# One GpSimd operation for the sum and one for the product of 1024 tokens, and a new order of all queues, in a gated recurrence with a gated convolution

## The chip, the cores and the metric

The kernel runs on one core of a Trainium2 chip. The metric is the device time of one execution in microseconds (us). TensorE is PE in the profile, VectorE DVE, ScalarE ACT, GpSimd POOL, SyncE SP; SPq is SyncE's queue, which issues the transfers.

## What is computed

The inputs are x, r_gate and i_gate, each of 4 sequences of 6336 tokens with 256 channels in float32. A linear recurrence with gates runs along each sequence; a gated linear unit with a causal convolution over 5 tokens follows.

```python
log_a = 8.0 * sigmoid(r_gate) * log(clip(sigmoid(a_param), 1e-6, 1 - 1e-6))
a_t = exp(log_a)
norm = sqrt(maximum(1 - a_t * a_t, 1e-6))
x_gated = norm * sigmoid(i_gate) * x
h = a_t[:, t] * h + x_gated[:, t]            # for every t; y[:, t] = h
gate = sigmoid(sum_k conv_w[k] * shifted(y, k))
out = (gate * (y @ w_val)) @ w_out
```

## The kernel before

The 25344 tokens are cut into windows (w) of 512 tokens, the last of 256, and the windows into chunks (c): chunks 0, 1 and 25 have one window of 512, chunk 26 the one of 256, and all others two, so that chunk c from 2 to 24 holds windows 2c-2 and 2c-1. Output is made by window; the last window is cut into windows 49 and 50 of 128.

Every piece of work is a word in one long list, `ORDER`, written out in the kernel. A word such as `sc.9.1` calls `op_sc(9, 1)`, and `@4,5` names the PSUM banks that it uses. Each engine does its words in the order of the list, one after the other; there is no other scheduling. The words of a chunk, in the order in which data flows:

- `lr`, `li`, `lx` (SyncE): load 512 KB of r_gate, i_gate or x of a window. Each ring has four windows, so a load waits until the window four places earlier was consumed.
- `ta.c`, `tb.c` (ScalarE): tanh of half of r and of i, in bfloat16. `tr.c.h` (TensorE) transposes the first for one half h of the channels, for two chunks at a time, and `ex.c.h` (ScalarE) makes the decays a_t from it.
- `sq.c.h` squares the decays on GpSimd; `sa` does the same on ScalarE. `rt.b.k` (ScalarE) takes the square roots for a batch of up to four chunks in one or two operations, since it needs another activation table: `rt.3` is for chunks 4 to 7, `rt.4` for 8 to 11, and so on; `rt.4.0` is for chunks 8 and 9. `rd` does this for chunk 0 on VectorE. `nt.c` (TensorE) transposes the roots.
- `pp.w` and `up.w` (GpSimd): tanh plus one, in place, and its product with x, for one window. In five windows `xp` (TensorE) and `uv` (VectorE, two instructions) do this instead.
- `xg.c` (VectorE) multiplies that by the root; `xt.c.h` (TensorE) transposes it; `sc.c.h` (VectorE) is the scan of the recurrence.
- `cv.w` (convolution), `vl.w` (x times w_val) and `ou.w` (output product) are TensorE's; `tg.w` (ScalarE) is the gate's tanh, `gv.w` (VectorE) the gate times the value. `cd.w` (VectorE) or `ca.w` (ScalarE) copies the output out of PSUM, and `st.w` (SyncE) stores it.

In the profile's lines: L310 is `ta`, L313 `tb`, L320 `pp`, L332 `up`, L346 `uv`, L373 `ex`, L381 `sq`, L389 `sa`, L406 `rt`, L441 `nt`, L452 and L456 `xg`, L466 `xt`, L499 `sc`, L511 `cv`, L518 `tg`, L526 `vl`, L531 `gv`, L541 `ou`, L549 `cd`, L551 `ca`, L562 `st`, L292 the loads.

Of the kernel before, what the change touches and what calls it, by code (L numbers as in the profile page):

```python
# [9 lines left out]
P = 128  # L10
CONV_K = 5
# [15 lines left out]
NU = 10  # L27
NRI = 4
NX = 4
# [20 lines left out]
xt.1.1@6 xt.2.1@0 sc.1.1 tg.0 li.9 sc.2.1 li.8 ex.4.1 vl.0@4,5 xt.2.0@1 tr.4.0@6,7 tb.4 gv.0 sq.5.1 cv.1@2,3 sc.2.0  # L50
ex.4.0 li.11 pp.5 lx.7 xp.4@4,5 lx.6 pp.6 uv.4 ta.6 pp.7 nt.3@6,7 up.5 ou.0.0@0,1 ta.7 lr.14 cv.3@4,5 cd.0.0 li.10
sq.5.0 lx.9 xg.3 tg.3 cv.2@0,1 lr.15 tg.1 lx.8 st.0 vl.1@6,7 sq.4.1 tg.2 xt.3.1@4 gv.1 tb.5 tr.6.0@0,1 sc.3.1 up.7
tr.6.1@6,7 ex.6.0 vl.2@2,3 up.6 lx.11 gv.2 li.12 ou.1.0@4,5 ex.6.1 lr.17 cd.1.0 xt.3.0@2 lr.16 sq.4.0 lx.10 sc.3.0
li.13 tb.6 ou.2.0@6,7 sq.7.0 vl.3@0,1 ta.8 li.15 cv.4@4,5 gv.3 sq.6.1 cd.2.0 tg.4 lr.18 ou.3.0@2,3 cd.3.0 sq.7.1
xp.8@0,1 lx.12 uv.8 rt.3.0 li.14 vl.4@2,3 st.1 sq.6.0 gv.4 lr.19 xp.9@6,7 uv.9 pp.11 lx.13 ou.4.0@2,3 rt.3.1 pp.10
cd.4.0 st.2 nt.4@6,7 up.10 xg.4 nt.5@0,1 xg.5 xt.4.0@4 up.11 lx.14 sc.4.0 xt.5.0@3 nt.6@6,7 tb.7 xt.4.1@2 sc.4.1
vl.5@0,1 ta.9 cv.5@4,5 li.16 pp.12 pp.13 xg.6 tg.5 lr.21 up.12 lr.20 tb.8 gv.5 li.17 tr.8.0@6,7 lx.15 sc.5.0 xt.6.1@0
up.13 lx.16 ex.8.0 xt.5.1@1 li.18 li.19 tr.8.1@4,5 sc.5.1 nt.7@2,3 pp.14 ex.8.1 st.3 ou.5.0@6,7 sq.9.0 st.4 ta.10 xg.7
cv.8@4,5 lx.17 up.14 cd.5.0 cv.6@2,3 tg.8 sc.6.1 xt.6.0@1 tg.6 pp.15 vl.6@4,5 ta.11 cv.7@2,3 sq.8.1 gv.6 cv.9@6,7 tg.7
lr.24 sc.6.0 up.15 lr.25 tb.9 st.5 ou.6.0@2,3 lr.23 tr.10.0@4,5 sq.8.0 cd.6.0 tg.9 vl.7@0,1 ex.10.0 st.6 gv.7 vl.8@2,3  # L60
lx.19 pp.16 xt.7.1@6 li.20 gv.8 xt.7.0@7 sq.9.1 tb.10 tr.10.1@0,1 sc.7.1 ou.7.0@4,5 sq.11.0 ex.10.1 cv.10@2,3 li.23
cd.7.0 tg.10 cv.11@0,1 sq.11.1 sc.7.0 st.7 ta.13 lr.22 lx.18 ou.8.0@4,5 li.21 pp.17 li.22 vl.9@2,3 tg.11 cd.8.0 sq.10.1
lr.29 gv.9 vl.11@4,5 sq.10.0 st.8 rt.4.0 gv.11 vl.10@0,1 ou.9.0@6,7 gv.10 up.17 cd.9.0 ou.10.0@0,1 rt.4.1 cd.10.0 up.16
ou.11.0@6,7 cd.11.0 st.10 nt.8@2,3 lr.28 pp.19 lx.21 xg.8 nt.9@0,1 lx.20 pp.18 xg.9 xt.8.1@3 cv.12@6,7 up.18 sc.8.1
ta.12 xt.8.0@5 up.19 tg.12 lr.26 sc.8.0 nt.10@2,3 lr.27 tb.11 st.9 tr.12.1@6,7 xt.9.1@1 xg.10 cv.14@4,5 ex.12.1 li.24
pp.20 li.25 sc.9.1 lx.22 pp.21 vl.14@2,3 lx.23 tg.14 cv.13@6,7 sq.13.1 tb.12 gv.14 vl.12@4,5 up.21 gv.12 tg.13
tr.12.0@0,1 li.26 st.11 vl.13@2,3 ex.12.0 li.27 pp.22 gv.13 ou.14.0@4,5 up.20 ou.12.0@6,7 cd.14.0 ta.15 ou.13.0@2,3
cd.12.0 xt.10.1@0 xt.9.0@1 ta.14 sq.12.1 lr.33 cd.13.0 cv.15@6,7 sc.9.0 tg.15 pp.23 lr.30 nt.11@4,5 lr.32 tb.13 up.22
lr.31 tr.14.0@2,3 lx.25 xg.11 st.12 tr.14.1@6,7 lx.24 ex.14.0 sc.10.1 cv.17@4,5 up.23 li.28 xt.10.0@1 tg.17 cv.16@2,3
st.13 sc.10.0 sq.14.0 ex.14.1 st.14 vl.17@4,5 pp.25 tg.16 lx.26 gv.17 vl.16@0,1 sq.15.1 tb.14 vl.15@6,7 gv.16 li.29  # L70
xt.11.0@2 gv.15 pp.24 cv.18@0,1 ta.17 sq.14.1 sc.11.0 ou.15.0@4,5 ta.16 ou.16.0@6,7 sq.12.0 cd.15.0 cv.19@2,3 tg.18
cd.16.0 st.15 xt.11.1@4 sq.13.0 tg.19 lr.37 lx.27 sc.11.1 li.30 vl.18@6,7 li.31 sq.15.0 ou.17.0@0,1 rt.5.0 gv.18
vl.19@4,5 up.25 gv.19 ou.18.0@6,7 cd.18.0 up.24 rt.5.1 ou.19.0@4,5 cd.17.0 nt.12@2,3 cd.19.0 pp.26 lx.28 nt.13@6,7
lx.29 xg.12 pp.27 cv.20@4,5 lr.36 st.17 up.26 xg.13 st.16 xt.12.0@3 tg.20 sc.12.0 tr.16.0@6,7 tb.15 up.27 lx.30
vl.20@0,1 lr.35 xt.12.1@4 lr.34 gv.20 ex.16.0 li.32 tr.16.1@2,3 li.33 pp.28 sc.12.1 st.18 nt.14@0,1 up.28 ex.16.1 lx.31
cv.21@6,7 xg.14 st.19 xt.13.1@5 tb.16 pp.29 sc.13.1 vl.21@2,3 sq.17.1 cv.22@0,1 tg.21 li.34 xt.13.0@4 li.35 tg.22 gv.21
pp.30 ou.20.0@6,7 ta.19 cv.23@0,1 sc.13.0 up.30 ca.20.0 vl.22@2,3 xt.14.0@5 up.29 tg.23 gv.22 ou.21.0@6,7 ta.18
cv.25@0,1 cd.21.0 sq.17.0 sc.14.0 tb.17 ou.22.0@2,3 lr.38 lr.39 tr.18.0@6,7 sq.16.0 st.20 lr.40 tg.25 cd.22.0 nt.15@4,5
# [31 lines left out]
def kernel(  # L110
# [80 lines left out]
    with tc.manual_schedule():  # L191
# [89 lines left out]
        def place(w, n):  # L281
            return w % n
# [327 lines left out]
```

## Time and profile before

| | us |
|---|---|
| three timed runs | 281.42, 281.95, 282.34; median 281.95 |
| span of the profiled execution | 279.6 |
| busy: DVE, ACT, PE, POOL | 258.2, 267.0, 243.8, 233.0 |
| DMA | 104.75 MB, mean 375 GB/s |

The profile gives the span of the profiled execution, from its first instruction to its last; its time as the timed runs measure it is not given apart. An engine's busy time is a mean over stages, so the stretches of the span are to be read beside it. A row of groups has the line, the engine, the operation and its shapes, the count, then busy us and mean ns of one, then the idle time of the engine before them and what ended it.

### The profile page before, as it was taken

What the parts mean: (1) busy time and instruction counts of PE and PEld (TensorE: products, weight loads), DVE (VectorE), ACT (ScalarE), POOL (GpSimd) and SP (SyncE); (2) the same over time, 40 slices, a digit from 0 to 9 for tenths busy, and PEclk for the clock granted to TensorE, in tenths of its full rate; (3) what the DMA queues carried; (4) which work ended last, traced back from release to release, by engine and by line L of the source; (5) the groups of instructions that cost most, each with busy time, mean ns of one, the idle gap of its engine ahead of it and who ended that gap; (6) DMA issues with size and microseconds to landing.
All of it is one profiled execution on the core that took longest, in us unless ns stands there. A gap on an engine that the chain in (4) does not pass through costs nothing. (4 is left out here: it accounts for less than half of the span.)

```text
span 279.6 us, 6233 instructions
## 1 busy us (share of the span) xinstructions
PE 243.8 (87%) x2493; PEld 164.9 (59%) x2493; DVE 258.2 (92%) x221; ACT 267.0 (96%) x187; POOL 233.0 (83%) x152
## 2 busy tenths in 40 slices
PE   2368999898799779999889999899999899999994
PEld 2143566456647466874566575666675756856563
DVE  5587797899999999899999999999999999999992
ACT  5999999999999999999999999999999999999754
POOL 1569679997999998999999999999999977984200
PEclk9998899999999999999999999999999999999999
DMA  7999999999999999999999999999999999742765
GB/s 275 411 405 385 388 409 409 413 409 409 419 408 417 415 414 416 413 416 409 420 413 341 415 420 414 414 411 420 416 363 407 420 378 400 286 176 92 283 263 194
DMA packets 29563, 104.75 MB, mean 375 GB/s; under 512 B 3287, under 2 KB 4062, under 8 KB 29534
## 3 DMA queue, kind: packets, MB, share of 16 engines
q1 hardware_dynamic: 29520, 104.35, 94.4%
q8 instruction: 19, 0.31, 0.4%
q14 instruction: 10, 0.08, 0.1%
q10 hardware_dynamic: 14, 0.01, 0.0%
HBM read 78.39 MB, written 25.95 MB: 373 GB/s over the span
## 5 line engine op out<-in xcount | busy, mean ns | idle before, releaser
L381 POOL TENSOR_TENSOR ering<-aring 128x1024 f32<-128x1024 f32 (+1 forms) x51 | 90.7, 1799 | 13.8 <-ACT aring L373 13.7
L332 POOL TENSOR_TENSOR uring<-tbring,xring 128x1024 bf16<-128x1024 bf16 (+1 forms) x45 | 95.5, 2139 | 3.2 <-DMA xring<-in_x_dram 1.7
L499 DVE TENSOR_TENSOR_SCAN yring<-aring,yring,banks 128x1024 bf16<-128x1024 f32 (+4 forms) x46 | 96.8, 2116 | 0.8 <-PE banks L466 0.7
L511 PE MATMUL banks<-yring,diag 64*64 64x512 bf16 (+6 forms) x1080 | 63.1, 362 | 3.8 <-ACT aring L373 1.1
L531 DVE SCALAR_TENSOR_TENSOR tgring<-tgring,banks 128x1024 bf16<-128x1024 bf16 (+1 forms) x51 | 59.4, 1178 | 6.1 <-PE banks L526 5.1
L320 POOL TENSOR_SCALAR tbring<-tbring 128x1024 bf16<-128x1024 bf16 (+1 forms) x45 | 46.3, 1040 | 10.3 <-ACT tbring L313 10.3
L541 PE MATMUL banks<-wo,tgring 128*128 128x256 bf16 x396 | 50.9, 273 | 4.4 <-DVE tgring L531 2.1
L373 ACT ACTIVATE aring<-banks,khf 128x2048 f32<-128x2048 bf16 (+3 forms) x32 | 52.9, 1689 | 0.2 <-PE banks L357 0.2
L526 PE MATMUL banks<-yring,wv 128*128 128x512 bf16 (+4 forms) x216 | 50.1, 361 | 2.7 <-DVE oring L549 1.0
L518 ACT ACTIVATE tgring<-banks 128x1024 bf16<-128x1024 f32 (+1 forms) x51 | 50.6, 1011 | 0.8 <-PE banks L511 0.6
L541 PEld LDWEIGHTS <-tgring 128*128 128x128 bf16 x396 | 42.3, 114 | 14.2 <-DVE tgring L531 5.8
L310 ACT ACTIVATE taring<-rring 128x2048 bf16<-128x2048 f32 (+2 forms) x27 | 47.9, 1785 | 1.7 <-DMA rring<-in_r_gate_dram 1.7
L313 ACT ACTIVATE tbring<-iring 128x2048 bf16<-128x2048 f32 (+2 forms) x27 | 48.1, 1782 | 0.0
L511 PEld LDWEIGHTS <-diag 64*64 64x64 bf16 x1080 | 29.4, 105 | 27.7 <-issue 12.5
L406 ACT ACTIVATE ering<-ering 128x4096 bf16<-128x4096 f32 (+3 forms) x14 | 43.6, 3157 | 0.1
L549 DVE COPY oring<-banks 128x1024 f32<-128x1024 f32 (+1 forms) x34 | 39.9, 1189 | 0.4 <-PE banks L541 0.4
L357 PE MATMUL banks<-ident_b,taring 128*128 128x128 bf16 x396 | 29.4, 230 | 8.5 <-ACT taring L310 4.5
L466 PE MATMUL banks<-ident,uring 128*128 128x128 f32 x198 | 30.3, 279 | 4.4 <-DVE uring L452 1.6
L357 PEld LDWEIGHTS <-taring 128*128 128x128 bf16 x396 | 26.0, 103 | 12.3 <-issue 6.3
L526 PEld LDWEIGHTS <-wv 128*128 128x128 bf16 x216 | 19.1, 97 | 23.8 <-issue 10.2
L466 PEld LDWEIGHTS banks<-ident,uring 128*128 128x128 f32 x198 | 21.9, 141 | 14.5 <-DVE uring L452 3.4
L441 PEld LDWEIGHTS banks<-ident,ering 128*128 128x128 f32 x184 | 24.2, 208 | 6.8 <-issue 3.0
(52 smaller groups left out, 160.0 us busy)
## 6 DMA issues: line engine op xcount, KB each, us to landing
rring<-in_r_gate_dram SPq DMA_DIRECT2D x49, 512.0 KB, 8.4
iring<-in_i_gate_dram SPq DMA_DIRECT2D x49, 512.0 KB, 9.0
xring<-in_x_dram SPq DMA_DIRECT2D x49, 512.0 KB, 9.4
out_dram<-oring SPq DMA_DIRECT2D x49, 512.0 KB, 9.0
oring<-in_moe_w_val_dram SPq DMA_DIRECT2D x1, 256.0 KB, 8.9
rring<-in_r_gate_dram SPq DMA_DIRECT2D x1, 256.0 KB
iring<-in_i_gate_dram SPq DMA_DIRECT2D x1, 256.0 KB, 6.5
xring<-in_x_dram SPq DMA_DIRECT2D x1, 256.0 KB
```

Source lines behind the costliest of these rows:

```text
L313: nc.scalar.activation(**tangent(c, tbring, NTI, iring, NII))
L332: nc.gpsimd.tensor_tensor(out=u, in0=t1, in1=xt, op=ALU.mult)
L357: nc.tensor.transpose(out=bank[:, o:o + P], in_=taring[:, place(w, NTR), j, h * P:(h + 1) * P], identity=ident_b[:])
L373: nc.scalar.activation(out=dst, in_=src, func=ACT.Exp, scale=khf[:, h:h + 1], bias=khf[:, h:h + 1])
L381: nc.gpsimd.tensor_tensor(out=e, in0=a, in1=a, op=ALU.mult)
L466: nc.tensor.transpose(out=out[:, o + q:o + wins[w] // 2:nq], in_=uring[:, w % NU, q, h * P:(h + 1) * P, :].rearrange("p d two -> p (d two) ...
L499: nc.vector.tensor_tensor_scan(out=yring[:, h, col:col + o1 - o0], data0=aring[:, h, a_at[c] + o0:a_at[c] + o1], data1=xT[:, o0:o1], initi ...
L511: nc.tensor.matmul(out=gp[oh * 64:oh * 64 + 64, h, a:b], lhsT=diag[half * 64:half * 64 + 64, h, k, :], rhs=yring[half * 64:half * 64 + 64, ...
L518: nc.scalar.activation(out=tgring[:, w % NTG, :, 0:outs[w]], in_=live.pop(("gp", w))[:, :, 0:outs[w]], func=ACT.Tanh, scale=0.5)
L526: nc.tensor.matmul(out=val[:, m, a:b], lhsT=wv[:, hk, m * P:(m + 1) * P], rhs=yring[:, hk, col:col + b - a], start=(hk == 0), stop=(hk == ...
L531: nc.vector.scalar_tensor_tensor(out=tgring[:, w % NTG, :, 0:outs[w]], in0=tgring[:, w % NTG, :, 0:outs[w]], scalar=1.0, in1=live.pop(("va ...
L541: nc.tensor.matmul(out=ops[:, j * D:(j + 1) * D], lhsT=gv[:, hk, j:outs[w]:J], rhs=wo[:, hk, :], start=(hk == 0), stop=(hk == H - 1))
```

## The change

In chunks 4, 6 to 24 (but not 5) the two sums `pp` and the two products `up` become one sum `pq.c` and one product `uq.c` over both windows, 2048 columns each. Chunks 1 to 3 and windows 8, 9, 48 and 49 keep the old words (chunk 5 is windows 8 and 9, done by `xp` and `uv` in both).

```diff
+        def op_pq(c):
+            w, k = cwins[c][0], len(cwins[c])
+            t = tbring[:, place(w, NTI):place(w, NTI) + k, 0:wins[w] // P, :].rearrange("p k j d -> p (k j d)")
+            nc.gpsimd.tensor_scalar(out=t, in0=t, scalar1=1.0, scalar2=1.0, op0=ALU.mult, op1=ALU.add)
+
+        def op_uq(c):
+            w, k = cwins[c][0], len(cwins[c])
+            nc.gpsimd.tensor_tensor(
+                out=uring[:, w % NU:w % NU + k].rearrange("p k q d two -> p (k q) two d"),
+                in0=tbring[:, place(w, NTI):place(w, NTI) + k].rearrange("p k (q two) d -> p (k q) two d", two=2),
+                in1=xring[:, w % NX:w % NX + k].rearrange("p k (q two) d -> p (k q) two d", two=2), op=ALU.mult)
```

The words `s_kt` and `s_diag` of the start are split into `s_ktp`, `s_ktd` and `s_dgp`, `s_dgc`, `s_dgd` with the same instructions. `op_vl` may use one bank for a short window. An `op_sb` is defined and not used. The three words `sa.21.1`, `sa.26.0` and `sa.26.1` become `sq`. `ca.20`, `ca.30`, `ca.50` become `cd`, and `cd.28`, `cd.40`, `cd.49` become `ca`.

The whole of `ORDER` is new, with its banks. All rings and their sizes, the chunks, the batches and the places of decays and squares stay. The stretch around chunks 3 to 8, before:

```
... tb.4 gv.0 sq.5.1 cv.1@2,3 sc.2.0 ex.4.0 li.11 pp.5 lx.7 xp.4@4,5 lx.6 pp.6 uv.4 ta.6 pp.7 nt.3@6,7 up.5 ou.0.0@0,1
ta.7 lr.14 cv.3@4,5 cd.0.0 li.10 sq.5.0 lx.9 xg.3 tg.3 cv.2@0,1 lr.15 tg.1 lx.8 st.0 vl.1@6,7 sq.4.1 tg.2 xt.3.1@4 gv.1
tb.5 tr.6.0@0,1 sc.3.1 up.7 tr.6.1@6,7 ex.6.0 vl.2@2,3 up.6 lx.11 gv.2 li.12 ou.1.0@4,5 ex.6.1 lr.17 cd.1.0 xt.3.0@2
lr.16 sq.4.0 lx.10 sc.3.0 li.13 tb.6 ou.2.0@6,7 sq.7.0 vl.3@0,1 ta.8 li.15 cv.4@4,5 gv.3 sq.6.1 cd.2.0 tg.4 lr.18
ou.3.0@2,3 cd.3.0 sq.7.1 xp.8@0,1 lx.12 uv.8 rt.3.0 li.14 vl.4@2,3 st.1 sq.6.0 gv.4 lr.19 xp.9@6,7 uv.9 pp.11 lx.13
ou.4.0@2,3 rt.3.1 pp.10 cd.4.0 st.2 nt.4@6,7 up.10 xg.4 nt.5@0,1 xg.5 xt.4.0@4 up.11 lx.14 sc.4.0 ...
```

and after:

```
... ou.1.0@0,1 sq.4.0 uv.4 tb.4 nt.3@2,3 cd.1.0 ou.0.0@6,7 sq.5.0 ta.6 cv.3@4,5 xg.3 st.1 pq.4 cd.0.0 xt.3.1@2 tg.3
cv.2@0,1 sc.3.1 ta.7 st.0 sq.4.1 lx.8 vl.3@4,5 li.10 li.11 xt.3.0@3 tg.2 lx.9 vl.2@6,7 gv.3 sq.5.1 tb.5 tr.6.0@0,1 gv.2
uq.4 sc.3.0 ex.6.0 tr.6.1@6,7 li.12 lr.16 ou.3.0@4,5 ex.6.1 cd.3.0 cv.4@2,3 ou.2.0@4,5 sq.7.0 lx.11 tg.4 st.3 vl.4@0,1
cd.2.0 tb.6 xp.8@6,7 sq.6.0 gv.4 st.2 lr.17 ou.4.0@2,3 sq.7.1 cv.5@0,1 rt.3.0 cd.4.0 uv.8 sq.6.1 xp.9@2,3 st.4 lr.15
lx.10 lr.14 li.13 pq.6 uv.9 lx.13 rt.3.1 nt.4@4,5 li.14 nt.5@2,3 xg.4 li.15 xg.5 xt.4.0@7 vl.5@4,5 lx.12 sc.4.0
nt.6@2,3 tg.5 uq.6 ta.9 gv.5 xt.4.1@7 xt.5.1@1 sc.4.1 ou.5.0@4,5 ta.8 cd.5.0 tb.7 cv.6@6,7 lr.19 xg.6 st.5 lr.18 tg.6
pq.7 lr.20 sc.5.1 vl.6@2,3 lr.21 tb.8 li.17 tr.8.0@6,7 lx.15 uq.7 gv.6 ex.8.0 xt.5.0@1 tr.8.1@4,5 sc.5.0 ou.6.0@2,3
ex.8.1 nt.7@6,7 xt.6.0@0 cd.6.0 sq.9.0 ta.10 cv.9@4,5 xg.7 st.6 lx.14 cv.7@2,3 sq.8.1 li.16 sc.6.0 tg.9 li.18 li.19
cv.8@6,7 ta.11 lr.23 lx.17 pq.8 xt.6.1@1 sc.6.1 tg.8 tr.10.0@4,5 lr.24 sq.8.0 tg.7 vl.7@6,7 ex.10.0 vl.8@2,3 gv.7 uq.8
tr.10.1@0,1 gv.8 ou.7.0@6,7 tb.9 ou.8.0@2,3 cd.7.0 vl.9@4,5 ex.10.1 cd.8.0 st.7 cv.11@6,7 sq.11.0 gv.9 st.8 xt.7.1@2
tb.10 li.20 lx.18 sc.7.1 cv.10@4,5 sq.9.1 lx.16 lr.25 tg.11 ou.9.0@0,1 tg.10 sq.10.1 cd.9.0 vl.10@2,3 vl.11@4,5 gv.10
st.9 sq.11.1 lx.19 xt.7.0@6 rt.4.0 lr.22 gv.11 ou.10.0@0,1 sq.10.0 cd.10.0 sc.7.0 ou.11.0@0,1 st.10 li.21 pq.9 rt.4.1
li.22 nt.8@4,5 xg.8 ...
```

More of the change, by code (lines that the diff above doesn't have):

```diff
@@ L50 @@
[L50 to L54, printed above, removed]
@@ L106 @@
+ca.48.0 vl.50@6 vl.49@1 gv.50 tg.49 st.48 ou.50.0@7 gv.49 cd.50.0 ou.49.0@5 st.50 ca.49.0 st.49
 """
@@ L381, in op_sq, with op_sb @@
             nc.gpsimd.tensor_tensor(out=e, in0=a, in1=a, op=ALU.mult)
+        def op_sb(c):
+            at, n = H * e_at[c], clen[c]
+            a = aring[:, :, a_at[c]:a_at[c] + n]
+            nc.gpsimd.tensor_tensor(out=ering[:, at:at + H * n].rearrange("p (h n) -> p h n", h=H), in0=a, in1=a,
+                                    op=ALU.mult)
         def op_sv(c, h):
```

134 lines of the change are left out of this document (71 added, 63 removed).

## The prediction

> **What bounds the kernel now.** I read the page's head first, then busy time by stretch, then who waited for whom, then the single instructions around the places that the new order moves.
>
> ```profile
> span 279.6 us, 6233 instructions
> PE 243.8 (87%) x2493; PEld 164.9 (59%) x2493; DVE 258.2 (92%) x221; ACT 267.0 (96%) x187; POOL 233.0 (83%) x152
> ```
>
> The profiled span is 279.6 us; the three timed runs have a median of 281.95. The 2.35 us between them I take as what lies around the span, and keep it. Below, a sum is made on the span and 2.35 is added. A difference under 0.3% (0.85 us) is what a measurement of this kernel can hardly tell from none.
>
> ```profile
> 20.00:40.00 20.00, 17.59 (x119) 9.78 (x118) 15.42 (x16) 19.94 (x12) 15.81 (x13) 0.91 1.03 392
> 40.00:80.00 40.00, 34.53 (x332) 23.91 (x331) 37.38 (x31) 39.76 (x25) 38.31 (x23) 1.00 1.03 411
> 80.00:240.00 160.00, 148.52 (x1605) 102.34 (x1604) 158.53 (x121) 159.77 (x106) 154.31 (x95) 1.00 1.02 407
> 240.00:260.00 20.00, 19.74 (x211) 12.68 (x210) 20.00 (x16) 19.93 (x22) 14.70 (x11) 1.00 0.49 174
> 260.00:280.00 20.00, 15.81 (x182) 10.43 (x182) 13.83 (x16) 10.89 (x13) 1.11 (x1) 0.97 0.58 230
> ```
>
> Columns: stretch, length, then PE, PEld, DVE, ACT, POOL busy, granted clock, DMA share, GB/s. From 80 to 240 us VectorE is idle for 1.5 us (160 - 158.53) and ScalarE for 0.2; the DMA engines are full as well (1.02) and ease only after 240. GpSimd, whose work the change cuts, has 5.7 us to spare there. Three resources are therefore full together, and GpSimd is not among them. VectorE's queue holds the same operations before and after (only which output copies it takes differs), so to end earlier the kernel must shrink VectorE's idle: 4.6 us in 20 to 40, 2.6 in 40 to 80, 1.5 in 80 to 240, and the tail.
>
> ```profile
> POOL ering L381 <- ACT aring L373: 13.7, 6, 6.6
> POOL tbring L320 <- ACT tbring L313: 10.3, 5, 4.1
> SPq L562 <- ACT oring L551: 27.2, 10, 5.3
> SPq L562 <- DVE oring L549: 22.0, 10, 10.3
> xring<-in_x_dram SPq DMA_DIRECT2D x49, 512.0 KB, 9.4
> DMA to landing us min/median/max: 3.6/8.9/10.9
> ```
>
> GpSimd waits for ScalarE, so it follows and does not lead. SyncE's queue (SPq) stood 49 us at stores (L562) for their copies; every load behind such a store waits too. A load of x takes 9.4 us to land at the median (last column), and any load between 3.6 and 10.9.
>
> **The change part by part.**
>
> ```profile
> L332 POOL TENSOR_TENSOR uring<-tbring,xring 128x1024 bf16<-128x1024 bf16 x44 | 94.3, 2161 | 2.8 <-DMA xring<-in_x_dram 1.3 <-PE banks L526 0.7
> L332 POOL TENSOR_TENSOR uring<-tbring,xring 128x512 bf16<-128x512 bf16 x1 | 1.2, 1180 | 0.4 <-DMA xring<-in_x_dram 0.4
> L320 POOL TENSOR_SCALAR tbring<-tbring 128x1024 bf16<-128x1024 bf16 x44 | 45.7, 1049 | 6.2 <-ACT tbring L313 6.2
> L320 POOL TENSOR_SCALAR tbring<-tbring 128x512 bf16<-128x512 bf16 x1 | 0.6, 620 | 4.1 <-ACT tbring L313 4.1
> L381 POOL TENSOR_TENSOR ering<-aring 128x1024 f32<-128x1024 f32 x45 | 84.6, 1900 | 6.2 <-ACT aring L373 6.1
> L389 ACT ACTIVATE ering<-aring 128x1024 f32<-128x1024 f32 x1 | 1.1, 1107 | 0.0
> L389 ACT ACTIVATE ering<-aring 128x256 f32<-128x256 f32 x2 | 0.9, 438 | 0.0
> L551 ACT COPY oring<-banks 128x1024 f32<-128x1024 f32 x16 | 16.4, 1025 | 4.3 <-PE banks L541 4.3
> L549 DVE COPY oring<-banks 128x1024 f32<-128x1024 f32 x33 | 39.4, 1213 | 0.4 <-PE banks L541 0.4
> L531 DVE SCALAR_TENSOR_TENSOR tgring<-tgring,banks 128x1024 bf16<-128x1024 bf16 x49 | 58.5, 1209 | 4.0 <-PE banks L526 3.6
> L499 DVE TENSOR_TENSOR_SCAN yring<-aring,yring,banks 128x1024 bf16<-128x1024 f32 x38 | 88.2, 2336 | 0.1
> L406 ACT ACTIVATE ering<-ering 128x4096 bf16<-128x4096 f32 x11 | 39.4, 3614 | 0.1
> ```
>
> *The merged operations.* From 512 to 1024 columns the product grows by 981 ns, the sum by 429. So 2048 columns should cost 2161 + 2 x 981 = 4.12 us and 1049 + 2 x 429 = 1.91 us; two of each now cost 4.32 and 2.10. That is 0.39 us a chunk, 7.8 us over 20 chunks, and at least nothing if 2048 columns cost just twice as much. It is off the path, since VectorE and ScalarE set the pace: I put 0 in the sum. If GpSimd were last ahead of an `xg`, 0.39 us would be won there.
>
> A rule speaks against even that saving. The Trainium skill, GPSIMD Engine Reference, section 3.1, gives 4497 ns for a two-input operation of 2048 columns in fp32; at that price the product of a chunk would lose 0.18 us instead of winning 0.20, and the cut on GpSimd would be about 0.2 us in all instead of 7.8. No row of this trace has a 2048-column product; the sum for the end would stay the same, since neither is on the path.
>
> *Squares.* Three squares go from ScalarE (`sa`, 1.11 + 2 x 0.44 = 2.0 us) to GpSimd: 1.90 for `sq.21.1`, and by length about 0.5 (an estimate from the same row) for each of the two of 256 columns. GpSimd's busy time should so go from 233.0 to about 228 (-7.8 + 2.9). ScalarE is full, but VectorE is equally full with unchanged work, so I take 0 of the 2.0 us; bound -2.0.
>
> *Copies.* Which of the output copies ScalarE takes changes (three against three, of equal sizes): no work is won or lost, VectorE carries one more copy, 1.21 us, until late and one less at the end.
>
> *Start.* `xp.0` now sits in banks 2,3, which `ex.2.0` frees first. But VectorE's list up to `xg.4` is the same set in both orders, and `xg.4` also needs `rt.3.0`:
>
> ```profile
> 54.27 1.94 ACT L310 ACTIVATE taring<-rring 128x2048 bf16<-128x2048 f32 x1
> 58.43 7.13 ACT L406 ACTIVATE ering<-ering 128x4096 bf16<-128x4096 f32 x2
> 51.63 9.31 POOL L381 TENSOR_TENSOR ering<-aring 128x1024 f32<-128x1024 f32 x5
> 63.77 2.35 DVE L452 TENSOR_TENSOR uring<-banks,uring 128x2048 bf16<-128x2048 bf16 x2
> ```
>
> The first row is `ta.8`, which moves behind `rt.3`: `rt.3` could run 1.9 us earlier, and `xg.4` (63.77) with it. But `rt.3.1` needs the last square (51.63 + 9.31 = 60.94), and GpSimd has the same squares, sums and products before that point. Bounds -1.9 and 0; I take -0.5, nearer to none because of that square.
>
> *Loads behind stores.* This is the part I give most weight. SyncE issues in order. Before, one store (`st.0`) stands ahead of `lx.10`; now five do (`st.1 st.0 st.3 st.2 st.4`), and `st.4` waits for `cd.4`. And `uq.6` needs `lx.10` and `lx.11` both, where the old products took one window each.
>
> ```profile
> 52.44 0.33 SPq L292 DMA_DIRECT2D xring<-in_x_dram  x1
> 58.60 1.35 DVE L346 SCALAR_TENSOR_TENSOR uring<-tbring,banks 128x512 bf16<-128x512 bf16 x2
> 61.25 1.39 DVE L346 SCALAR_TENSOR_TENSOR uring<-tbring,banks 128x512 bf16<-128x512 bf16 x2
> 102.77 2.35 DVE L452 TENSOR_TENSOR uring<-banks,uring 128x2048 bf16<-128x2048 bf16 x2
> ```
>
> `lx.10` is issued at 52.44 now. In the new order `cd.4` stands just ahead of `uv.8` and `uv.9` (1.35 + 1.39) and `xg.4` (63.77), so it ends near 61.0; with `st.4` and `lr.15` issued between, `lx.10` goes out near 62.0, ten us later. With a 9.4 us landing, `uq.6` (4.12) ends at 75.5. `xg.6` stands on VectorE behind `xg.4 xg.5` (2.35), two scans (2 x 2.34), `gv.5` and `cd.5` (2 x 1.21), about 9.1 us with the overlaps of some 0.08 each that the x2 rows show: 72.9. So `uq.6` is 2.6 us late; with the shortest landing, 3.6, it is 3.2 us early.
>
> The same happens at `lx.14`, now behind `st.6` and so behind `cd.6`: from 72.9, `xg.6`, two scans, `gv.6` and `cd.6` end near 80.8, `lx.14` goes out at 81.2. With 9.4 us, `uq.8` ends at 94.7. Behind it on GpSimd wait five squares, of which the second ends at 98.5 and releases `rt.4.0` (3.61): 102.1, and transposes still follow. `xg.8` is now at 102.77 and would be reached at 101.6, since one copy moved behind it: 0.5 late without the transposes, about 1.0 with them (my estimate); 0 with the short landing. ScalarE's own slack does not help there, because it waits for the squares.
>
> Together 0 to 3.6 us. While SyncE stands at a store fewer transfers are in flight, so the landing should fall below the median 8.9, yet 8.9 is nearer to what the trace shows most often than 3.6. At 7.5 us the first is 0.7 late and the second nothing; at 8.9, 2.1 and 0.5. I take 1.2.
>
> *Banks and the rest of the order.* A new order moves VectorE's small waits about. Its idle now is 2.6 us in 40 us (40 to 80) and 1.5 in 160. I take +0.5 more, with bounds -1.5 (all idle from 80 to 240 gone) and +2.6 (one more stretch like 40 to 80).
>
> *Tail.*
>
> ```profile
> 250.89 3.29 ACT L406 ACTIVATE ering<-ering 128x2048 bf16<-128x2048 f32 x2
> 253.19 1.22 DVE L456 TENSOR_TENSOR uring<-banks,ering 128x2048 bf16<-128x2048 bf16 x1
> ```
>
> `xg.24` (253.19) starts as `rt.8.0` is done and VectorE comes free. Now one copy more and `gv.41` less stand ahead of it: 1.21 - 1.21 = 0. ScalarE has 3.0 us less ahead of `rt.8` (2.0 of squares, one copy of 1.02), but VectorE would not be there sooner. From here the matmuls are the same, TensorE being busy 19.74 of the 20 us before 260. I take 0, with VectorE's one copy (1.2) as bound on both sides.
>
> Sum: -0.5 + 1.2 + 0.5 + 0 = +1.2. Span 280.8, and 2.35 around it: 283.2 us (rounded).
>
> **The rivals.**
>
> *Slow landings decide (slower still).* Both x waits at their full 9.4 us, 2.6 + 1.0, and +1.0 for the order, with -0.5 at the start: +4.1, 286.0 us. For it: the DMA share of 1.02 up to 240 us, so that nothing late can be made up; sums and products of both windows now wait for the later x. Against it: a standing queue means fewer transfers in flight. It decides from a landing of about 8.9 us on.
>
> *ScalarE was the true limit (faster).* It is idle for only 0.2 us between 80 and 240, less than VectorE's 1.5. Then its 2.0 us of squares come off the end, with the -0.5 of the start: 281.95 - 2.5 = 279.5 us. For it: ScalarE's 96%. Against it: VectorE would have to lose 2.5 of its idle, and between 80 and 240 it has only 1.5. It decides if VectorE's idle from 40 to 80 falls below about 1 us.
>
> *Nothing moves.* The landing is under 6.8 us, so both x waits vanish, and the order's +0.5 cancels the start's -0.5: 281.95, within 0.3%. That the merged operation does not save what it says belongs here: even then nothing ends later, as long as GpSimd keeps its 5.7 us of slack.
>
> A sentence that stands apart: the Trainium skill, DMA: Bandwidth & Descriptors, section on the anatomy of one DMA, has a fixed 2.0 us and 436 GB/s, an estimate of 3.2 us for 512 KB, and by it this rival would be the forecast (281.95); the trace's shortest, 3.6, is near, but its median of 8.9 under a full load speaks against it.
>
> **How the numbers follow.** Forecast (283.2): 0.38. Slow landings (286.0): 0.22. ScalarE the limit (279.5): 0.26. Nothing moves: 0.14. Faster 0.26, same 0.14, slower 0.60. The range reaches down to the faster rival's own price, 279.5, and up past the slow one by one more us of idle, 287.0; outside lie half of the faster case's 0.26 and a quarter of the slow case. Forecast alone: 282.8 to 285.
>
> **What would show it.** Right: VectorE idle just ahead of `xg.6` or the scans of chunk 6, or of `xg.8`, released by GpSimd or through it by `in_x_dram`; the GpSimd product of 128x2048 waiting for x in total well over 2.8 us; SPq's waits at L562 above 49 us; GpSimd's busy time near 228 to 230. The product of 2048 columns near 4.12 us confirms the merging, near 4.5 or over denies it. Wrong: VectorE idle below 1 us in 40 to 80 and the span below 279, or waits of VectorE that come from ScalarE's square roots in mid-kernel, or a tail over 25 us after `rt.8`.

## The result and the profile after

| | us |
|---|---|
| changed kernel, 4 runs | 285.51 to 287.63, median 286.37 |
| kernel before, 4 runs on the same chip | 281.42 to 282.34, median 281.92 |
| ratio | 1.0164, 95% interval 1.0136 to 1.0192 |
| profiled execution of the changed kernel | 286.28, its span 284.3 |

The change makes the kernel slower by 4.45 us, and the span longer by 4.7. 286.37 lies in the range and on the side that the forecast gave; the forecast's +1.2 us is too small, and the runs below show that its largest term names the wrong cause. In all that follows, an execution more than 1.5% above the fastest of the same kernel is left out of times and ratios; the only one is the profiled execution of the run with `lx.10` moved (289.77).

The head of the page after, then the busy time by stretch (the columns of the prediction's table), and two groups of GpSimd:

```profile
span 284.3 us, 6194 instructions
PE 243.5 (86%) x2493; PEld 164.7 (58%) x2493; DVE 258.3 (91%) x221; ACT 267.1 (94%) x184; POOL 229.9 (81%) x115
```

```profile
20.00:40.00 20.00, 14.85 (x119) 9.15 (x119) 15.56 (x17) 18.41 (x12) 15.80 (x12) 0.91 1.03 399
40.00:80.00 40.00, 34.97 (x316) 23.68 (x315) 36.54 (x30) 39.54 (x23) 32.68 (x15) 1.00 1.00 394
80.00:240.00 160.00, 144.80 (x1574) 99.52 (x1574) 155.68 (x119) 157.28 (x100) 152.71 (x65) 0.99 1.02 403
240.00:260.00 20.00, 19.73 (x212) 13.44 (x210) 19.95 (x15) 19.68 (x20) 18.87 (x11) 1.00 0.59 211
```

```profile
L346 POOL TENSOR_TENSOR uring<-tbring,xring 128x2048 bf16<-128x2048 bf16 x20 | 82.5, 4126 | 10.0 <-DVE yring L522 5.8 <-DMA xring<-in_x_dram 2.0 <-PE banks L565 0.9
L342 POOL TENSOR_SCALAR tbring<-tbring 128x2048 bf16<-128x2048 bf16 x20 | 38.0, 1901 | 2.5 <-ACT tbring L318 2.5
```

VectorE has the same work as before (258.3 against 258.2), ScalarE too (267.1 against 267.0), so the new time is idle time of both (on ScalarE with a reservation, given below under *Squares*). Between 80 and 240 us VectorE's idle grows from 1.5 to 4.3 us and ScalarE's from 0.2 to 2.7; from 20 to 40 ScalarE loses 1.5 more. The merged operations themselves came out as worked out, 4.13 and 1.90 us.

The waits after, of SyncE's queue and then of ScalarE (us in total, times, longest), and last ScalarE's wait for the convolutions before:

```profile
SPq L586 <- DVE oring L573: 65.5, 27, 5.0
SPq L586 <- ACT oring L575: 35.5, 13, 8.7
```

```profile
ACT tgring L541 <- PE banks L534: 4.7, 7, 1.4
ACT taring L315 <- DMA rring<-in_r_gate_dram: 2.4, 4, 1.3
ACT aring L390 <- PE banks L374: 1.0, 2, 0.8
```

```profile
ACT tgring L518 <- PE banks L511: 0.6, 2, 0.4
```

SyncE now stands 101 us at stores, where it was 49: what the forecast feared is there, and the tempting reading is that this is the loss. ScalarE waits 4.7 us for convolutions on TensorE (L534), against 0.6 before. Which of the two counts is what the runs had to tell.

An account of ScalarE says where the time went. It is worked out from all its records from its first tangent, at 4.3 us, on: work, and gaps of more than 0.12 us between two instructions, loads of the activation table (1.3 each, the same number in both orders) included in the gaps.

```
ahead of      before: start  work   idle     after: start  work   idle
rt.3.0                 58.4   49.5   4.55            58.9   48.2   6.38
rt.5.0                138.2  124.1   9.79           141.6  124.6  12.68
rt.6.0                175.8  159.0  12.42           181.2  160.0  16.80
rt.8.0                250.9  228.9  17.67           255.1  228.1  22.56
last instruction      276.9  247.6  24.88           281.7  247.6  29.60
```

(The last row's "start" is its end.) Work 247.6 in both, idle +4.72, end +4.8: by these records the change is idle time to a tenth. 1.83 us of it arise ahead of `rt.3.0`, 1.06 up to `rt.5.0`, 1.49 up to `rt.6.0`, 0.51 up to `rt.8.0`, and after it none. These are one execution of each kernel. The same account of the two runs with half the stores (below), which have the same two orders, gives 0.85 ahead of `rt.3.0` (5.15 and 6.00) and 2.12 from there to `rt.8.0`, so the shares are good to about 1 us.

### The profile page after: what moved, and what is told of

Same layout as the page of the kernel before. It is cut to its first block, busy times and chain, and to the rows that moved or that the text cites. A ratio compares the mean times of both kernels' runs of the same rounds, so it can differ in the third digit from the quotient of the medians.

```text
span 284.3 us, 6194 instructions
## 1 busy us (share of the span) xinstructions
PE 243.5 (86%) x2493; PEld 164.7 (58%) x2493; DVE 258.3 (91%) x221; ACT 267.1 (94%) x184; POOL 229.9 (81%) x115
## 2 busy tenths in 40 slices
DMA packets 29562, 104.74 MB, mean 368 GB/s; under 512 B 3287, under 2 KB 4062, under 8 KB 29534
## 5 line engine op out<-in xcount | busy, mean ns | idle before, releaser
L398 POOL TENSOR_TENSOR ering<-aring 128x1024 f32<-128x1024 f32 (+2 forms) x54 | 93.2, 1750 | 9.4 <-ACT aring L390 9.4
L346 POOL TENSOR_TENSOR uring<-tbring,xring 128x2048 bf16<-128x2048 bf16 x20 | 82.5, 4126 | 10.0 <-DVE yring L522 5.8
L534 PE MATMUL banks<-yring,diag 64*64 64x512 bf16 (+6 forms) x1080 | 63.0, 362 | 4.6 <-DVE yring L522 3.0
L565 PEld LDWEIGHTS <-tgring 128*128 128x128 bf16 x396 | 41.2, 115 | 18.0 <-DVE tgring L555 8.7
L550 PE MATMUL banks<-yring,wv 128*128 128x512 bf16 (+4 forms) x216 | 49.5, 361 | 2.2 <-DVE uring L475 1.0
L315 ACT ACTIVATE taring<-rring 128x2048 bf16<-128x2048 f32 (+2 forms) x27 | 47.3, 1767 | 2.4 <-DMA rring<-in_r_gate_dram 2.4
L534 PEld LDWEIGHTS <-diag 64*64 64x64 bf16 x1080 | 28.9, 106 | 28.2 <-issue 12.7
L342 POOL TENSOR_SCALAR tbring<-tbring 128x2048 bf16<-128x2048 bf16 x20 | 38.0, 1901 | 2.5 <-ACT tbring L318 2.5
L374 PE MATMUL banks<-ident_b,taring 128*128 128x128 bf16 x396 | 29.7, 230 | 9.6 <-ACT taring L315 7.4
L374 PEld LDWEIGHTS <-taring 128*128 128x128 bf16 x396 | 25.9, 103 | 14.6 <-ACT taring L315 9.1
L464 PE MATMUL banks<-ident,ering 128*128 128x128 f32 x184 | 27.9, 300 | 5.7 <-ACT ering L429 4.3
L464 PEld LDWEIGHTS banks<-ident,ering 128*128 128x128 f32 x184 | 25.4, 209 | 11.2 <-ACT ering L429 4.4
```

What stands on the lines that cost most here:

```text
L346: nc.gpsimd.tensor_tensor(out=uring[:, w % NU:w % NU + k].rearrange("p k q d two -> p (k q) two d"), in0=tbring[:, place(w, NTI):place(w, ...
L374: nc.tensor.transpose(out=bank[:, o:o + P], in_=taring[:, place(w, NTR), j, h * P:(h + 1) * P], identity=ident_b[:])
L398: nc.gpsimd.tensor_tensor(out=e, in0=a, in1=a, op=ALU.mult)
L464: nc.tensor.transpose(out=bank[:, k:k + P], in_=ering[:, e + q:e + wins[w] // 2:nq], identity=ident[:])
L534: nc.tensor.matmul(out=gp[oh * 64:oh * 64 + 64, h, a:b], lhsT=diag[half * 64:half * 64 + 64, h, k, :], rhs=yring[half * 64:half * 64 + 64, ...
L550: nc.tensor.matmul(out=val[:, m, a:b], lhsT=wv[:, hk, m * P:(m + 1) * P], rhs=yring[:, hk, col:col + b - a], start=(hk == 0), stop=(hk == ...
```

## Experiments: the merge

**The merge without the new order, the new order without the merge.** Each run is compared with the kernel before on its own chip. Its median there was 281.43 us for these two, for `lx.10` and for the start; 281.55 for the sums, the products, the five loads and the square; 281.40 for the 58 loads and the half stores; 281.63 for the four waits.

```diff
  order before, chunks 4 and 6 to 24 only:
- pp.10 ... pp.11        up.10 ... up.11
+           pq.6                   uq.6        (at the place of the second)
```

> The order of before in full (its copies, its squares on ScalarE, its banks); only the sums and products of the 20 chunks are merged, each standing where the second of the two stood. Theory A (the merged operation itself is harmless, as GpSimd was not last): 281.4 to 282.4 us, VectorE idle as before (about 1.5 us from 80 to 240). Rival B (holding both x windows until the end of the longer product delays the loads): 283.5 us or more, with waits of GpSimd for in_x_dram well over 2 us.

Measured: 284.79 us (283.63 to 286.28), ratio 1.0122 (1.008 to 1.0163): +3.4.

```diff
  new order:
- pq.6       uq.6
+ pp.10 pp.11      up.10 up.11
```

> The order of after in full; only the merged sums and products are taken apart again, into two adjacent operations per chunk. Theory A (the order costs the time): 285.8 to 287.2 us, no gain, at most 0.4 us lost to 7 us more work on GpSimd. Rival B (the merging costs the time): 284 us or less.

Measured: 288.98 (286.61 to 289.83), ratio 1.0254 (1.0205 to 1.0303): 2.6 us slower than the changed kernel and 7.5 slower than before.

That is above both expected ranges. So the two halves of the change don't add. The merge costs 3.4 us in the order before, and is worth 2.6 us in the new one, which was made for it (3.1 if each is compared with the kernel before on its own chip); the new order costs 7.5 us without the merge, and next to the merge in the old order about 1.1 by the same comparison (1.6 between the medians, 286.37 and 284.79). That the merge lies off the path, the theory I began with, is refuted.

**Which merge, and through what.** First only the sums, then only the products:

> The order before, with only the sums of a chunk put together (at the place of its first sum); the products stay apart by window, and so an x buffer still comes free after its own window's product. Theory X (the merge costs because a merged product starts only when both x windows are there and frees both only at its end): 281.5 to 282.3, nothing against the kernel before. Rival G (any GpSimd operation of 2048 columns costs, because it holds up the squares and the first window behind it): some 0.9 us per sum on the first product of a chunk, 282.6 to 283.5.

> The order before, with only the products of a chunk put together (at the place of its second product); the sums stay apart. Theory X: the whole +3.4 of the merge in that order, 284.3 to 285.3. Rival G: about two thirds of it, since the product has two thirds of the merged time, 283.5 to 284.3, with the rest in the run of the sums.

Measured: sums only 281.62 (ratio 1.0006, 0.9983 to 1.0029), nothing. Products only 286.06 (284.58 to 287.49; ratio 1.0158, 1.0107 to 1.0209): the whole cost, and no less than with both (the intervals overlap), if above the 284.3 to 285.3 that theory X named. It is the product, as theory X said; that any GpSimd operation of 2048 columns costs (rival G) is refuted by the sums.

A product of one window gives its x buffer free after 2.16 us; the merged product gives two at its end, after 4.13. The loads that wait for them stand in SyncE's queue, in order. SyncE from 224 us, the order before and then the merge in that order (start, length with the wait in it):

```profile
224.34 2.94 SPq L292 DMA_DIRECT2D xring<-in_x_dram  x2
227.34 0.42 SPq L562 DMA_DIRECT2D out_dram<-oring  x1
227.81 0.46 SPq L292 DMA_DIRECT2D xring<-in_x_dram  x1
```

```profile
226.47 6.25 SPq L296 DMA_DIRECT2D xring<-in_x_dram  x2
232.76 0.43 SPq L585 DMA_DIRECT2D out_dram<-oring  x1
233.24 2.63 SPq L296 DMA_DIRECT2D xring<-in_x_dram  x1
```

and that queue's waits for products, before and with the merge:

```profile
SPq L292 <- POOL uring L332: 11.6, 8, 5.0
```

```profile
SPq L296 <- POOL uring L345: 25.7, 7, 5.5
```

The second load of the first row is `lx.46`. It waited to 227.0 for `up.42`, and waits now to 232.4 for `uq.22`; `lx.45`, behind it in the queue though its own buffer was free at 226.3, is begun at 233.24 instead of 227.81, and its issue takes 2.63 us instead of 0.46. In all, SyncE waits 25.7 us for merged products (before, 11.6 for the single ones). GpSimd then waits for `lx.45`, which lands at 240.2:

```profile
228.23 4.13 POOL L345 TENSOR_TENSOR uring<-tbring,xring 128x2048 bf16<-128x2048 bf16 x1
233.49 1.90 POOL L341 TENSOR_SCALAR tbring<-tbring 128x2048 bf16<-128x2048 bf16 x1 [1.13 <-ACT tbring L317]
240.47 4.13 POOL L345 TENSOR_TENSOR uring<-tbring,xring 128x2048 bf16<-128x2048 bf16 x1 [5.09 <-PE banks L373]
```

The row names TensorE as the releaser, but 240.47 is 0.25 us after that landing. From `uq.23` to the end of `uq.24` (256.4) GpSimd has no gap; the transposes of chunk 24 on TensorE start 0.05 us behind it, and VectorE stands 1.49 us ahead of `xg.24`, where it had no gap before:

```profile
257.64 1.23 DVE L478 TENSOR_TENSOR uring<-banks,ering 128x2048 bf16<-128x2048 bf16 x1 [1.49 <-PE banks L488]
```

This is one place of several. ScalarE was 1.7 us late at `rt.4.0` already (98.7 for 97.0) and 2.3 at `rt.7.0`; at `rt.8.0` it is 2.9 late (253.8 for 250.9). To test that the queue is the way, five loads were put behind what they held up:

```diff
  the queue of SyncE (likewise lx.16, lx.19, lx.30):
- lx.11 li.12 lr.17 lr.16
+ li.12 lr.17 lr.16 lx.11
- lx.46 st.34 lx.45 st.35 li.46
+ st.34 lx.45 st.35 li.46 lx.46
```

> The merge in the order before (284.8), with five loads of x that waited for a merged product at the head of SyncE's queue put behind the loads and stores that they held up (lx.11, lx.16, lx.19, lx.30, lx.46). If the queue behind a waiting load is where the +3.4 comes from: 282.0 to 283.0. If it is the merged product's own late start and end (both x windows needed, both u windows later), with the queue of little account: 284.0 to 285.0.

Measured: 282.29 (281.46 to 283.06), ratio 1.0029 (1.0015 to 1.0044). Five words take back 2.5 of the 3.4 us. SyncE's waits for merged products fall to 11.4 us, and the hole ahead of `uq.23` to 2.86:

```profile
SPq L296 <- POOL uring L345: 11.4, 4, 5.6
```

```profile
236.73 4.12 POOL L345 TENSOR_TENSOR uring<-tbring,xring 128x2048 bf16<-128x2048 bf16 x1 [2.86 <-DVE tgring L554]
```

So most of the merge's cost is the queue behind a load that waits for the later of two buffers, and with those five loads moved the merge costs 0.3%, about what can just be told from nothing. The kernel before wasn't run with the same loads moved, so what they would win there isn't known; ScalarE has 0.2 us of idle left in it between 80 and 240 us.

## Experiments: the new order

In the new order SyncE waits little for merged products, so that way is closed there, and +4.45 remain to be explained:

```profile
SPq L297 <- POOL uring L346: 4.2, 4, 1.7
```

**Loads behind stores.** First the one load that the prediction named, `lx.10`, put ahead of the last three of its five stores:

> The order of after with one word moved: lx.10 stands right behind lx.11, ahead of the stores st.3, st.2 and st.4. The 5.8 us that GpSimd stood ahead of uq.6 should shrink to under 1.5. Theory L (loads behind stores, the forecast's largest term): 284.0 to 285.2 us. Theory S (ScalarE late from the start): within 0.5 us of after, 285.9 to 286.8, since uq.6 was just in time for xg.6 and ScalarE reaches rt.5 no sooner.

Measured: 284.99 to 286.52, ratio 1.0172 (1.0154 to 1.0189). No gain, though the 5.8 us of GpSimd ahead of `uq.6` were gone (0.08, in the profiled execution). Then all of them: 58 loads whose buffer was free go ahead of the store that held them up.

```diff
  the queue of SyncE around 45 to 70 us; all other engines unchanged:
- st.1 st.0 lx.8 li.10 li.11 lx.9 li.12 lr.16 lx.11 st.3 st.2 lr.17 st.4 lr.15 lx.10 lr.14 li.13 lx.13 li.14 li.15 lx.12 ...
+ ... lx.8 li.10 li.11 lx.9 st.0 li.12 lr.16 lx.11 st.3 lr.17 lr.15 lx.10 lr.14 st.2 li.13 li.14 li.15 lx.12 st.4 lx.13 ...
```

> The changed kernel; only SyncE's queue is rearranged: 58 loads whose buffer was already free, and which stood behind a store that was still waiting for its copy, go ahead of that store. All other engines keep their order. Theory Q (the new order's loss is loads issued late behind waiting stores, 101 us of such waits against 49): 282.0 to 284.0. Rival E (the loss is in the new order of ScalarE, VectorE and TensorE themselves): 286 to 287. A third way, H: the 4 us come from the data rate as such, and stores that go later only swap places with loads: 285 to 286.5.

Measured: 285.71 (285.19 to 286.34), ratio 1.0142 (1.0116 to 1.0168). That is far above theory Q's 282 to 284, in the range of H and just below that of E. It is 0.7 us under the changed kernel, and the intervals overlap; against the kernel before on its own chip it is +4.3, where the change is +4.45. The hole of GpSimd that held the prediction's term does shrink, after and then here (the first row names a scan of VectorE, but `lx.10` landed 0.23 us before `uq.6` starts):

```profile
68.77 4.12 POOL L346 TENSOR_TENSOR uring<-tbring,xring 128x2048 bf16<-128x2048 bf16 x1 [5.77 <-DVE yring L522]
```

```profile
63.96 4.12 POOL L345 TENSOR_TENSOR uring<-tbring,xring 128x2048 bf16<-128x2048 bf16 x1 [1.62 <-DMA xring<-in_x_dram]
```

`uq.6` ends 4.8 us earlier, ScalarE's idle ahead of `rt.3.0` falls from 6.38 to 4.91, and the end hardly moves: ScalarE then waits 1.17 us for `lr.29` at 119 us (0.42 after the change).

**Is the data rate the limit?** Both kernels show a DMA share of 1.02 up to 240 us. Every store was cut to half of its rows (half the output stays unwritten), so 13 of 105 MB aren't moved, with all instructions and waits in place.

```diff
- nc.sync.dma_start(of[...].rearrange("(p j) d -> p j d", p=P), oring[:, w % NOSB, 0:J, :])
+ nc.sync.dma_start(of[...].rearrange("(p j) d -> p j d", p=P)[:, 0:max(1, J // 2)], oring[:, w % NOSB, 0:max(1, J // 2), :])
```

> The changed kernel, with every store writing only half of its rows (256 KB instead of 512 KB, half the output is left unwritten); all instructions, waits and orders stay, only 13 MB of 105 MB are not moved. If the new order loses its 4.4 us because the transfers bind (theories Q and H): 279 to 282, level with the kernel before under the same cut or below it. If it loses them in the order of the engines (rival E): 284 to 286, still 3 to 4.5 us over the kernel before under the same cut.

> The kernel before with the same cut: every store writes half of its rows. If the transfers hold the kernel before up too, next to ScalarE and VectorE: 279 to 281. If not: 281.5 to 282.2, no change, since VectorE stands only 1.2 us between 45 and 266 us. This run is the base for the other half-store run.

Measured: the order before 281.54 (ratio 0.9998, 0.9984 to 1.0012), the new order 285.2 (284.98 to 286.6; ratio 1.0137, 1.0099 to 1.0174). From 80 to 240 us, before and after with the cut:

```profile
80.00:240.00 160.00, 147.49 (x1590) 102.12 (x1602) 158.57 (x122) 159.76 (x106) 155.03 (x95) 1.00 0.94 349
```

```profile
80.00:240.00 160.00, 144.21 (x1563) 99.70 (x1580) 156.21 (x120) 157.65 (x101) 153.58 (x64) 0.99 0.97 357
```

With a seventh fewer bytes a second the kernel before gains nothing, and the new order keeps 3.7 of its 4.45 us. The landings got shorter as well (of x, 7.8 us at the median after the change and 6.8 with the cut). So neither the bytes nor the time to landing are what the new order loses its time to, but for about 0.8 us. The number of packets stayed as it was (29,562), and the DMA share is still near 1; a limit by packets was not tried by itself.

**ScalarE's waits.** What is left is the order of the engines among each other. Two places show it. At the start, ScalarE from 28 us, before and then after:

```profile
29.94 1.91 ACT L310 ACTIVATE taring<-rring 128x2048 bf16<-128x2048 f32 x1
31.76 1.90 ACT L313 ACTIVATE tbring<-iring 128x2048 bf16<-128x2048 f32 x1
33.56 1.00 ACT L518 ACTIVATE tgring<-banks 128x1024 bf16<-128x1024 f32 x1
```

```profile
30.65 1.02 ACT L541 ACTIVATE tgring<-banks 128x1024 bf16<-128x1024 f32 x1
31.57 1.90 ACT L315 ACTIVATE taring<-rring 128x2048 bf16<-128x2048 f32 x1
34.19 1.02 ACT L541 ACTIVATE tgring<-banks 128x1024 bf16<-128x1024 f32 x1 [0.72 <-PE banks L534]
35.11 1.90 ACT L318 ACTIVATE tbring<-iring 128x2048 bf16<-128x2048 f32 x1
37.82 4.02 ACT L390 ACTIVATE aring<-banks,khf 128x2048 f32<-128x2048 bf16 x2 [0.81 <-PE banks L374]
```

Before, ScalarE has two tangents from loads (L310, L313) to do before its first gate (L518), and no gap. After, two gates come early. The second waits for its convolution (L534), which on TensorE waited 1.37 us for a scan; a later exponential waits for its transposes (L374), which stand on TensorE behind that convolution: two gaps, 1.53 us together. The second place is the square root at 141 us. Before, ScalarE there, TensorE at `nt.12` and VectorE at `xg.12`, all without a gap:

```profile
138.20 7.13 ACT L406 ACTIVATE ering<-ering 128x4096 bf16<-128x4096 f32 x2
```

```profile
142.24 2.08 PE L441 MATMUL banks<-ident,ering 128*128 128x128 f32 x16
```

```profile
144.59 2.35 DVE L452 TENSOR_TENSOR uring<-banks,uring 128x2048 bf16<-128x2048 bf16 x2
```

After, ScalarE, then VectorE at `xg.12`, then TensorE at `nt.12`:

```profile
141.60 7.13 ACT L429 ACTIVATE ering<-ering 128x4096 bf16<-128x4096 f32 x2 [0.24 <-POOL ering L398]
150.99 1.02 ACT L541 ACTIVATE tgring<-banks 128x1024 bf16<-128x1024 f32 x1 [0.96 <-PE banks L534]
```

```profile
147.36 1.22 DVE L475 TENSOR_TENSOR uring<-banks,uring 128x2048 bf16<-128x2048 bf16 x1 [1.36 <-PE banks L464]
```

```profile
145.28 3.38 PE L464 MATMUL banks<-ident,ering 128*128 128x128 f32 x16 [2.79 <-ACT ering L429]
```

ScalarE comes to the root 3.4 us later than before; TensorE and VectorE have run out of other work, and then ScalarE waits for `cv.20`, which stands on TensorE behind the transposes of `xg.12`. In the order before, `cv.20` stood ahead of `xt.12`.

Two runs tried single causes. Giving the part up to 57 us back to the order before:

> The order of after, but the words up to tb.6 (the first 57 us or so) stand in the order and banks of before; lx.10 stays behind st.4. Theory S (ScalarE loses 2 us to waits in the first 40 us, is full from there on and arrives late at rt.5, where VectorE waits): 283.8 to 284.8 us, rt.5.0 starting 1.5 to 2.5 us earlier than the 141.6 of after. Rival L (the loads behind stores after 57 us make GpSimd and the squares late): 285.8 us or more, rt.5.0 within 0.7 us of 141.6. Rival P (GpSimd's own order of squares ahead of rt.5 sets it): ScalarE earlier, but rt.5.0 waits over 1 us for sq.13.1 and the time is 285.5 or more.

Measured: 290.28 (289.62 to 291.49), ratio 1.0319 (1.0289 to 1.0348). Slower still, and none of the three theories has its mark: `rt.5.0` starts at 143.9, 2.3 later than after the change, and doesn't wait for the square. `xg.4` starts at 66.5, 2.6 later than after the change; `uq.6` waits 6.41 us for x at the seam, but is done before VectorE comes to `xg.6`, which has no gap. What made VectorE late there wasn't followed up. The later part may be fitted to its own start; whether that start is good the run doesn't tell. And the square ahead of the root (`sq.13.1` behind `sq.13.0`):

> The changed kernel with one square (chunk 13, second half) moved on GpSimd from its place ahead of rt.5 to right behind the other half's, three merged operations earlier; nothing else changes. Theory P (the square root of 141 us, and with it xg.12 and the 1.4 us that VectorE stands still there, waits for GpSimd's order): 284.4 to 285.2. Rival S (ScalarE comes to that square root 3 us late by its own work, so that GpSimd's half is not what counts): 286.0 to 286.6.

Measured: 287.13 (286.51 to 287.39), ratio 1.0193 (1.0175 to 1.0212). Theory P falls, and the time is above rival S's 286.0 to 286.6 too. `rt.5.0` starts at 141.0, 0.6 earlier, and ScalarE's wait for `cv.20` grows from 0.96 to 2.26.

Last, four of ScalarE's waits were taken away together, on top of the loads ahead of the stores:

```diff
- lr.28 lr.27 lr.26 lr.29
+ lr.28 lr.29 lr.27 lr.26
- sq.13.0 pq.12 uq.12 ... pq.13 sq.13.1
+ sq.13.0 sq.13.1 pq.12 uq.12 ... pq.13
- cd.18.0 cd.19.0 sc.11.1      nt.12 nt.13 xt.12.1 xt.12.0 cv.20
+ sc.11.1 cd.18.0 cd.19.0      cv.20 nt.12 nt.13 xt.12.1 xt.12.0
- li.45 lr.47 li.44 st.31
+ st.31 li.45 lr.47 li.44
```

> The kernel with the loads ahead of the stores (285.7), with four waits of ScalarE taken away by order alone: lr.29 ahead of lr.27 and lr.26 (ScalarE waits 1.17 for it at 119 us); square 13.1 right behind 13.0 on GpSimd (0.23 and more ahead of rt.5.0); the scan sc.11.1 ahead of two output copies on VectorE and cv.20 into the hole of TensorE ahead of nt.12 (tg.20 waits 0.95 for it); the loads li.45, lr.47, li.44 back behind st.31 (ca.35 waits 0.64). Theory S (the new order's loss is ScalarE's idle time ahead of the last square root, to the microsecond): some 2.5 to 3.0 us of idle go, 282.6 to 283.4. Rival V (ScalarE's waits are symptoms; VectorE and TensorE, which wait at the same places, or another wait take their place): 284.8 to 286.

Measured: 285.06 (284.07 to 286.18), ratio 1.0127 (1.0106 to 1.0148). That is rival V's range. All four waits went, as this row of ScalarE shows for one (no gap, where 0.96 was), and `xg.12` starts at 144.1, 0.5 earlier than in the kernel before.

```profile
147.48 1.02 ACT L540 ACTIVATE tgring<-banks 128x1024 bf16<-128x1024 f32 x1
```

But the lead is used up behind it: VectorE and ScalarE get new waits, each at a place where they had none,

```profile
183.42 1.22 DVE L474 TENSOR_TENSOR uring<-banks,uring 128x2048 bf16<-128x2048 bf16 x1 [0.87 <-PE banks L463]
```

```profile
188.62 1.94 ACT L540 ACTIVATE tgring<-banks 128x1024 bf16<-128x1024 f32 x2 [0.61 <-PE banks L533]
...
242.03 1.06 ACT L317 ACTIVATE tbring<-iring 128x1024 bf16<-128x1024 f32 x1 [0.92 <-POOL uring L345]
```

and `xg.24` is at 255.8, 1.6 earlier than after the change and 2.7 later than before. Of the 3.3 us won at `xg.12`, 1.4 are left in the span (281.7 to 280.3 at the last work of ScalarE). So rival V holds and theory S doesn't: the account of idle time is right as an account, but a single wait of ScalarE is no price that one gets back.

**What stays open.** That the new order doesn't lose its time to bytes, or to loads late behind stores, is shown (half stores, loads ahead of stores). That it loses it in how the engines wait for each other is what is left, and the account of idle time fits it. Which choice in the order sets it isn't shown: four waits removed gave 0.65 us of the 4.3 that were left (285.71 to 285.06, with overlapping ranges); of the waits after `xg.12` only one was among them (ahead of `ca.35`), those at the end weren't tried, and no run takes the new banks apart from the new order. None of the versions beats the kernel before.

## Why the prediction was right, and where not

*Merged operations.* The prices were right: 4126 ns against 4.12 us, 1901 against 1.91. The 4497 ns that the Trainium skill, GPSIMD Engine Reference, section 3.1, gives for fp32 are not what this bfloat16 product takes; the row decides. GpSimd's busy time came to 229.9 (228 to 230 was named). What failed is the 0 on the path. I asked who waits for GpSimd's results, and found nobody; I did not ask who waits for the buffers that it frees. In the order before that is worth +3.4 us, and in the new one the split costs 2.6.

*Squares.* 0 of 2.0 us, right in result. But ScalarE's busy time didn't fall at all (267.0 and 267.1 with three instructions fewer). Its records add up to 284.3 us before and 280.2 after; neighbours in them overlap, by 17.3 us in all before and 13.2 after. So its instructions follow each other less closely in the new order, and that takes up the 2.0 us of squares and more: ahead of `rt.8.0` ScalarE's work fell by 0.8 us, where the prediction had 3.0. What makes the overlaps shorter is open, and no run took the squares apart.

*Copies.* 0, with no run that contradicts: VectorE's busy time is the same.

*Start, taken as -0.5.* The sign was wrong. `xg.4` is at 63.9 instead of 63.8, and behind that equality ScalarE has 1.3 us less done (48.2 against 49.5 ahead of `rt.3.0`, `ta.8` being moved) and 1.83 us more idle (0.85 between the two runs with half the stores). I had bounded the step by what `ta.8` frees, and had not gone through ScalarE's new order up to 40 us, where the two gates stand.

*Loads behind stores, taken as +1.2.* The direction of the waits came true (101 us for 49), and `lx.10` was issued at 61.1, where 62.0 was forecast. It landed in 7.5 us, not 9.4, and `uq.6` ended at 72.9 just as VectorE came to `xg.6` at 73.0: no stall. `lx.14` made none either. At most about 0.7 us of the result belongs to this step, by the run with 58 loads ahead; if the term was there, it was smaller, and not at the two places named. The reading that a queue with fewer in flight lands sooner was right (below).

*Banks and the rest of the order, taken as +0.5 with a bound of +2.6.* This is the term that was mis-sized. From `rt.3.0` to `rt.8.0` ScalarE has 3.06 us more idle (2.12 between the two runs with half the stores). I had sized it by VectorE's idle in the kernel before, which shows how well that order was packed, and not what a different one loses.

*Tail, 0.* From `xg.24` to the end of the span it was 26.4 us before and is 26.9 after: +0.5.

*Around the span.* The 2.35 us were too much: wherever this case has both for one execution, the time is 1.7 to 2.1 us over the span. The prediction had set the median of the timed runs against the span of another execution.

*The rivals.* The time came out near that of the slow landings (286.0), but not by their mechanism: landings got shorter. That the range, whose upper end comes from that rival, holds the result is luck as far as the cause goes. ScalarE as the limit is half right, without its sign: ScalarE is full in the kernel before and lost its time, and taking the squares off it won nothing. *Nothing moves* needed landings under 6.8 us; x took 7.8 at the median. The fit behind the 3.2 us that the prediction takes from the Trainium skill, DMA: Bandwidth & Descriptors, section on the anatomy of one DMA, is given there for transfers issued by GpSimd, and these are SyncE's. Of the marks, GpSimd's busy time, the store waits and the merged product's wait for x came true (10.0 us of idle ahead of it; 2.0 name x, and 5.8 ended just after `lx.10` had landed), although the loads were not the cause: they don't tell the forecast from what happened. A tail over 25 us after `rt.8` could tell nothing either, since it was 25.4 before the change (25.9 after). VectorE's wait for square roots in mid-kernel, which I had named as a mark against the forecast, is there at 147 us, and it was the better trace of the cause.

## What to carry to other kernels

When two operations become one, follow what they free as well as what they make: buffers come free in pairs and later, and in an in-order queue every load behind the first one that waits for them is late too; moving a handful of queue entries is then worth more than the merge. In an order in which two engines have no idle left, a new order is to be priced by going through each engine's list and asking at each word what it will wait for, above all at the start and around the batched steps; idle time in the old profile is no measure for it. And that the transfer engines are busy doesn't make them the limit: see whether moving fewer bytes makes the kernel faster.

## What the hardware showed unexpectedly

At a DMA share of 1.02 over 160 us, the 407 GB/s were no limit: with 13 MB fewer the same kernel ran in the same time (281.54 against 281.40), the share at 0.94 and 349 GB/s.

The median time to landing fell as the queue stood more. For the stores before, then for x and the stores after (x took 9.4 before):

```profile
out_dram<-oring SPq DMA_DIRECT2D x49, 512.0 KB, 9.0
```

```profile
xring<-in_x_dram SPq DMA_DIRECT2D x49, 512.0 KB, 7.8
out_dram<-oring SPq DMA_DIRECT2D x49, 512.0 KB, 6.2
```

A late issue is therefore partly made up on the way. That fits that 52 us more of store waits cost so little; it wasn't tried by itself.

The granted clock of TensorE was 0.91 in 140 to 160 us after the change, behind its 2.79 us of idle, where it had been 1.00 before; in the run with the square moved it was 0.83 there, with ScalarE idle 2.3 us of the 20. Whether the clock follows from the idle time was not tried by itself. It is not what the new order loses most of its time to: with the four waits removed it was 1.00 in that stretch, and the kernel was still 3.4 us slower than before.
